# Inverse root as a power on GpSimd, two more row additions on VectorE, more transposes by DMA

## Chip, cores and metric

The kernel runs on one core of a Trainium2 chip. The metric is the device time of one execution in microseconds (us). The engines are TensorE (PE, with its weight loads PEld), VectorE (DVE in the profile, `V` in the code), ScalarE (ACT, `A`), GpSimd (POOL, `G`) and SyncE (SP, `nc.sync`), which here only issues DMAs. A name with a q behind it (SPq, POOLq, ACTq) is the queue of such issues.

## What is computed

Attention over a sliding window of 128 with 4 sink columns, for 4 batches, 8 heads, 768 positions and head size 64, and then a gated MLP block with a spatial gate over the positions:

```python
keep = is_sink | in_window                       # 0 <= row - column < 128, or column < 4
a = softmax(where(keep, q @ k.T / 8, -1e9))
x = (a @ v), heads side by side                  # 4 x 768 x 512

h = gelu_tanh(x @ w_in)                          # 512 -> 1024
u, v = h[..., :512], h[..., 512:]
v_n = (v - mean(v)) / sqrt(var(v) + 1e-6) * g_ln
v_s = einsum('ts,bsd->btd', w_sg, v_n) + b_sg
out = x + (u * v_s) @ w_out                      # float32, 4 x 768 x 512
```

Inputs and output are float32; the matrix products run in bf16.

## The kernel before

Work is cut into 16 pairs of heads (n = 0 to 15; four pairs make one batch) and 4 MLP blocks (b = 0 to 3, one a batch). The positions are six tiles of 128 rows (`NT` = 6). The order on every engine is written out by hand: each engine runs its instructions in the order of the code, and the string `ORDER` (L717) with `INSIDE` (L712) lists the steps behind block 0.

A pair goes through these steps. `load` (L90) fetches k, q and v by DMA from SP's queue into three raw buffers of each name. `cast` (`ck`, `cq`, `cv`; L101) turns them to bf16 on GpSimd. q and k must then stand with the head dimension on partitions. `columns` (`KA`, `QA`, `QV`; L215) does that by six TensorE transposes and one copy on ScalarE or VectorE; `columns_by_dma` (`TD`; L228) does it by two DMA transposes on SP's queue. Which way a pair takes goes with the order of rows in its load: pairs from `FIRST` on (L88) are loaded row by row and turned by DMA. `score` (`S`; L251) multiplies and takes the exponential on ScalarE, `keep_band` (`m`; L283) sets entries outside the window to zero (group 0 on VectorE, the others on GpSimd), and `values` (`A0`, `A1`; L307) multiplies with v; VectorE divides by the sums, keeps the reciprocals in `rcps` and writes x. The x of a pair is turned for the MLP by TensorE (`turn_x`, `XV`; L337) or by a DMA transpose (`turn_x_by_dma`, `XD`; L352).

A block begins when its four pairs are there. `hidden` (L585) issues 14 units: six `hidden_v` (TensorE, GELU on ScalarE, mean and variance on VectorE) and eight `hidden_u`. Behind unit 7 comes `inverse_root` (L400), which gives 1/sqrt(var + 1e-6) for six values in each partition: a first guess from the bits and three Newton steps, 13 instructions on VectorE. `normalise` (L419) then writes the six tiles of `vn`. The rest of the block is put in a list of fillers that the steps `F` take from between the pairs of the next batch: eight `spatial` (L426; six matmuls, then `gv` and `gT` on VectorE), then six `project` (L458; one tile of 128 output rows each). `project` adds x either on TensorE, by a matmul with the identity, and copies with ScalarE (`by_act`), or it adds x on VectorE; a DMA then stores the rows. `LAST` steps of `INSIDE` run behind the last unit of a block, when `vn` is just being written. In this kernel the two rows that are projected there in each block (rows 3 and 5) are both `by_act`. For block 2 rows 3, 4 and 5 are projected behind the units of block 3, by `fill(3)`.

PSUM gives four banks (`ps_m`) to all of these steps but the scores; a bank is free again when the engine that reads it is done.

No pairs follow block 3. There `open_v` (L363) begins the first three `hidden_v` with the pairs whose x is turned already. `count_good` (L486) counts the reciprocals that are in a plain range, and `total` (L498) sums them over the partitions; if one is not, `general()` computes all again in a safe way. It does not run with these inputs. The last rows are projected by `project` and `project_last` (L440).

## Time and profile before

| | |
|---|---|
| median of 3 runs | 164.64 us (164.34 to 168.64) |
| profiled execution | 163.95 us, its span 162.2 us |
| busy share of the span | PE 94%, DVE 81%, ACT 67%, POOL 49% |
| granted TensorE clock, mean | 0.991 |
| moved by DMA | 31.11 MB, mean 192 GB/s |

The span runs from the first to the last event of the execution on the core; the time of the execution is a little longer. Rows of the trace give a start, a length, engine and line, the operation, what it writes and reads, and in brackets the idle time of the engine before it with what ended that. Lengths of pipelined instructions overlap, so the distance between the starts of two of them is the better price of one. Views that group instructions give the busy time and the mean length in nanoseconds. The view of waits gives the total time waited in us, how many times, and the longest.

### The profile page before, as it was taken

How to read it: one execution, taken by the hardware profiler on the slowest of the kernel's cores; microseconds unless marked ns; L12 is line 12 of the kernel's file. 1: busy time of each engine (PE TensorE's matmuls, PEld its weight loads, DVE VectorE, ACT ScalarE, POOL GpSimd, SP SyncE). 2: the span in 40 equal slices, each digit the busy share in tenths (PEclk: the TensorE clock that was granted, in tenths of full speed). 3: DMA queues.
4: the chain of work that ended last, by engine and by line, in shares of the span. 5: the costliest groups of instructions: out<-in, count | busy, mean ns of one | idle time of the engine just before them, and what ended most of it. 6: DMA issues, size and time to landing. Idle time of an engine off the chain costs nothing.

```text
span 162.2 us, 4449 instructions
## 1 busy us (share of the span) xinstructions
PE 152.6 (94%) x1753; PEld 90.5 (56%) x1753; DVE 131.5 (81%) x323; ACT 109.0 (67%) x148; POOL 79.5 (49%) x114
## 2 busy tenths in 40 slices
PE   3889999999999999999999999999999999999960
PEld 3446574666567666565566655554556645555530
DVE  6857975996999995799989984999999959888840
ACT  3198978879977689798977576679759457611020
POOL 6568680404999989641369949102985100000010
PEclk9999999999999999999999999999999999999996
DMA  4999979999999989999932899999932220031253
GB/s 131 337 341 256 210 99 254 223 293 311 304 234 320 297 235 337 317 233 219 188 113 53 119 239 159 261 232 218 216 73 49 111 87 0 0 147 51 91 208 107
DMA packets 60131, 31.11 MB, mean 192 GB/s; under 512 B 48356, under 2 KB 57080, under 8 KB 60104
## 3 DMA queue, kind: packets, MB, share of 16 engines
q1 hardware_dynamic: 56656, 27.20, 71.1%
q0 software_dynamic: 3024, 3.03, 11.1%
q10 hardware_dynamic: 424, 0.53, 1.0%
q8 instruction: 15, 0.25, 0.7%
q14 instruction: 12, 0.10, 0.2%
HBM read 24.81 MB, written 6.29 MB: 192 GB/s over the span
## 4 chain that ended last, share of the span: by engine, by line
PE 67%; DVE 20%; DMA 5%; issue 2%; SPq 1%; ACT 1%; POOL 1%; DVEq 0%; POOLq 0%; ACTq 0%
PE vs L432 14%; PE o_ps L464 9%; PE av L324 7%; PE hv L370 7%; PE sc L267 7%; PE hu L389 6%; DVE st L381 5%; DMA k_sb<-in_k_dram 5%; DVE vn L422 3%; PE xps L341 3%; DVE gv L435 2%; PE av L330 2%; PE kps L219 2%; PE qps L219 2%; PE hv L377 2%
## 5 line engine op out<-in xcount | busy, mean ns | idle before, releaser
L281 ACT ACTIVATE ex<-sc 128x1024 bf16<-128x1024 f32 x48 | 47.4, 1023 | 12.2 <-PE sc L267 6.3
L432 PE MATMUL vs<-wsgT,vn 128*128 128x384 bf16 x192 | 35.6, 326 | 0.2
L298 POOL TENSOR_SCALAR_AFFINE_SELECT ex<-ex 128x512 bf16<-128x512 bf16 x24 | 17.8, 743 | 14.2 <-ACT ex L281 10.3
L107 POOL CAST k_bf<-k_sb 128x768 bf16<-128x768 f32 x15 | 13.1, 871 | 24.0 <-DMA k_sb<-in_k_dram 21.2
L432 PEld LDWEIGHTS <-vn 128*128 128x128 bf16 x192 | 17.6, 97 | 10.9 <-DVE vn L422 0.7
L464 PE MATMUL o_ps<-w_out_sb,gT 128*128 128x512 bf16 x92 | 23.2, 380 | 0.1
L389 PE MATMUL hu<-xT,w_in_sb 128*128 128x384 bf16 x128 | 22.1, 327 | 0.0
L435 DVE SCALAR_TENSOR_TENSOR gv<-vs,g_sb,b_bc 128x384 bf16<-128x384 f32 x32 | 19.6, 612 | 2.2 <-PE vs L432 1.6
L381 DVE BATCH_NORM_STATS2 st<-v_all 128x6 f32<-128x512 f32 x24 | 16.1, 671 | 3.5 <-ACT v_all L379 3.5
L370 PE MATMUL hv<-w_in_sb,xT 128*128 128x512 bf16 x72 | 18.8, 379 | 0.0
L333 DVE TENSOR_TENSOR x<-av,rcps 128x384 bf16<-128x384 f32 x32 | 17.8, 558 | 1.1
L392 ACT ACTIVATE uT<-hu 128x384 bf16<-128x384 f32 x32 | 15.7, 492 | 4.1 <-PE hu L389 3.7
L379 ACT ACTIVATE v_all<-hv 128x512 f32<-128x512 f32 x24 | 13.2, 599 | 7.5 <-PE hv L377 7.1
L107 POOL CAST q_bf<-q_sb 128x768 bf16<-128x768 f32 x15 | 15.3, 1019 | 4.5 <-DMA q_sb<-in_q_dram 1.9
L438 DVE TENSOR_TENSOR gT<-gv,uT 128x384 bf16<-128x384 bf16 x32 | 15.5, 486 | 2.2 <-DVE gv L435 0.5
L389 PEld LDWEIGHTS <-w_in_sb 128*128 128x128 bf16 x128 | 12.3, 98 | 8.0
L472 ACT COPY o_sb<-o_ps 128x512 f32<-128x512 f32 x11 | 6.3, 593 | 15.4 <-PE o_ps L467 15.3
L267 PE MATMUL sc<-qT,kT 64*128 64x256 bf16 (+2 forms) x384 | 16.0, 256 | 0.5 <-DVE qT L225 0.4
L324 PE MATMUL av<-v_sb,ex 128*128 128x65 bf16 x352 | 16.1, 195 | 0.0
L324 PEld LDWEIGHTS <-ex 128*128 128x128 bf16 x352 | 13.0, 98 | 4.7 <-issue 1.9
L104 POOL CAST v_sb<-v_sb 128x768 bf16<-128x768 f32 x16 | 13.5, 842 | 3.2 <-DMA v_sb<-in_v_dram 3.2
L476 POOL DMA_DIRECT2D out_dram<-o_sb x1 | 0.6, 585 | 29.5 <-DVE o_sb L474 29.5
(91 smaller groups left out, 233.1 us busy)
## 6 DMA issues: line engine op xcount, KB each, us to landing
k_sb<-in_k_dram SPq DMA_DIRECT2D x16, 384.0 KB, 6.7
v_sb<-in_v_dram SPq DMA_DIRECT2D x16, 384.0 KB, 6.0
q_sb<-in_q_dram SPq DMA_DIRECT2D x15, 384.0 KB, 5.6
out_dram<-o_sb SPq DMA_DIRECT2D x22, 256.0 KB, 2.4
wsg_sb<-in_moe_w_sg_dram POOLq DMA_DIRECT2D x2, 576.0 KB, 11.6
w_in_sb<-in_moe_w_in_dram POOLq DMA_DIRECT2D x2, 256.0 KB, 5.1
w_in_sb<-in_moe_w_in_dram POOLq DMA_DIRECT2D x1, 512.0 KB, 5.4
w_out_sb<-in_moe_w_out_dram POOLq DMA_DIRECT2D x1, 512.0 KB, 9.2
```

The costliest lines, as they stand in the source:

```text
L107: eng.tensor_copy(dst.rearrange("p t (h d) -> p h t d", h=2), src)
L267: nc.tensor.matmul(sc[part, 512 * l + w:512 * l + w + n_q], kT[rows, 128 * j + wide * a:128 * j + wide * (a + 1)], qT[rows, 128 * j:128 * ...
L281: A.activation(out=exps[n][:, g, :], in_=sc, func=AF.Exp, scale=scale)
L298: eng.affine_select(out=diag, in_=diag, compare_op=ALU.is_ge, fill=0.0, base=0, pattern=[[0, 2], [0, 2], [1, 128]], channel_multiplier=-1)
L324: nc.tensor.matmul(av[:, m, l, :], probs(j, l, half), v_sb[:, l, j, :], start=first, stop=False)
L333: V.tensor_mul(x_sb[b][:, hp, HT * c:HT * (c + 1), :].rearrange("p i (l d) -> p i l d", l=2), av[:, :, :, 0:64], rcp.to_broadcast([128, HT ...
L370: nc.tensor.matmul(hvs[b, j], xT[b][:, c, 128 * j:128 * (j + 1)], w_in_sb[:, c, DF:], start=(c == 0), stop=False)
L381: V.bn_stats(out=st, in_=v_alls[b][:, j, :])
L389: nc.tensor.matmul(h_ps[:, 0:NH], w_in_sb[:, c, 128 * f:128 * (f + 1)], xT[b][:, c, NH * n:NH * (n + 1)], start=(c == 0), stop=(c == KD - 1))
L432: nc.tensor.matmul(vs[:, 0:NH], vns[b][:, si, 128 * f:128 * (f + 1)], wsgT[:, si, cols], start=(si == 0), stop=(si == NT - 1))
L435: V.scalar_tensor_tensor(out=gv, in0=vs[:, 0:NH], scalar=g_sb[:, f:f + 1], in1=b_bc[:, cols], op0=ALU.mult, op1=ALU.add)
L464: nc.tensor.matmul(o_ps, gTs[b][:, c, rows], w_out_sb[:, c, :], start=(c == 0), stop=(c == KU - 1 and not by_act))
```

## The change

- `inverse_root` keeps its first instruction on VectorE (w = var + 1e-6) and takes w to the power -0.5 in one GpSimd instruction, with a constant tile of -0.5.
- `by_act` holds only row 1: rows 3 and 5 of blocks 0 to 2 add x on VectorE, without the identity matmul and without ScalarE's copy.
- `FIRST` is 11: pair 11 (the twelfth) is loaded row by row and turned by `TD 11`; `KA 11` and `QA 11` go. kT and qT have three buffers in place of two.
- The x of pair 14 (the fifteenth) is turned by `XD 14` in place of `turn_x` on TensorE and ScalarE. `open_v` of block 3 takes the parts of pairs 12 and 13 first, then x of pair 15 is turned, and then the parts of pair 14 are added.
- The steps `TD` stand directly behind their casts; within block 1 `ck 11`, `cq 11` come behind unit 9, and `L 13` behind them and `TD 11`.
- `count_good` runs on GpSimd, a matmul pair and a small ScalarE copy sum over the partitions (`count_columns`), and a second matmul over the 96 columns; both stand inside the last block.
- In block 0 `turn_g` comes one unit after the last `hidden_v`, and the second of three `turn_weights` copies is VectorE's.
- Of block 3's rows, row 0 is stored from GpSimd's queue in place of row 3.

```diff
@@ -71,6 +71,7 @@
     off = consts.tile([128, 512], BF16, name="off")
     off0 = consts.tile([128, 512], BF16, name="off0")
     ones = consts.tile([128, 1], BF16, name="ones")
+    minus_half = consts.tile([128, NT], F32, name="minus_half")
 
     vst = [consts.tile([n_sink, c, 2, 65], BF16, name=f"vst{i}")
            for i, c in enumerate((HP, NP - HP))]
@@ -85,7 +86,7 @@
 
         nc.sync.dma_start(out=gates[:, i, :], in_=behind)
 
-    FIRST = 3 * HP
+    FIRST = 3 * HP - 1
 
     def load(n, which, eng=None, in_rows=False):
         b, hp = divmod(n, HP)
@@ -140,6 +141,7 @@
         V.memset(t[:, :, :, 64:65], 1.0)
     load_sinks(0)
     V.memset(ones, 1.0)
+    V.memset(minus_half, -0.5)
     for t in v_bufs:
         V.memset(t[:, :, :, 64:65], 1.0)
     V.memset(off, 0.0)
@@ -217,7 +219,7 @@
         ps = bank([128, NT, 128], BF16, which + "ps")
         for t in range(NT):
             nc.tensor.transpose(ps[:, t, :], src[:, t, :], iden)
-        dst = work.tile([128, S], BF16, name=which + "T")
+        dst = work.tile([128, S], BF16, name=which + "T", bufs=3)
         o, i = dst.rearrange("c (p t) -> c p t", t=NT), ps.rearrange("c t p -> c p t")
         if eng is A:
             A.copy(o, i)
@@ -229,7 +231,7 @@
 
         for which, Ts in (("k", kTs), ("q", qTs)):
             src = flat.pop((n, which))
-            dst = Ts[n] = work.tile([128, S], BF16, name=which + "T")
+            dst = Ts[n] = work.tile([128, S], BF16, name=which + "T", bufs=3)
             nc.sync.dma_start_transpose(out=dst.rearrange("c (t p) -> c t p", t=NT),
                                         in_=src.rearrange("p t c -> p (t c)"))
 
@@ -400,20 +402,9 @@
     def inverse_root(b):
 
         w = small.tile([128, NT], F32, name="w", bufs=2)
-        h = small.tile([128, NT], F32, name="h", bufs=2)
-        s = small.tile([128, NT], F32, name="s", bufs=2)
-        si = small.tile([128, NT], I32, name="si", bufs=2)
         y = small.tile([128, NT], F32, name="y", bufs=2)
         V.tensor_scalar(out=w, in0=mvs[b][:, :, 1], scalar1=1e-6, scalar2=None, op0=ALU.add)
-        V.tensor_single_scalar(out=si, in_=w.bitcast(I32), scalar=1,
-                               op=ALU.logical_shift_right)
-        V.tensor_scalar(out=h, in0=w, scalar1=-0.5, scalar2=None, op0=ALU.mult)
-        V.tensor_scalar(out=y.bitcast(I32), in0=si, scalar1=-1.0, scalar2=float(0x5f3759df),
-                        op0=ALU.mult, op1=ALU.add)
-        for _ in range(3):
-            V.tensor_mul(s, y, y)
-            V.tensor_mul(s, s, h)
-            V.scalar_tensor_tensor(out=y, in0=s, scalar=1.5, in1=y, op0=ALU.add, op1=ALU.mult)
+        G.tensor_tensor(out=y, in0=w, in1=minus_half, op=ALU.pow)
         rstds[b] = y
 
     def normalise(b, j):
@@ -483,23 +474,34 @@
 
     LEAST, MOST = 1e-20, 1e20
 
+    NR = NP * NT
+
     def count_good():
-        good = small.tile([128, NP * NT * 2], F32, name="good", bufs=1)
-        cnt = small.tile([128, 1], F32, name="cnt", bufs=1)
-        cnt_bf = small.tile([128, 1], BF16, name="cnt_bf", bufs=1)
+
+        big = small.tile([128, 2 * NR], F32, name="big", bufs=1)
+        good = small.tile([128, 2 * NR], F32, name="good", bufs=1)
+        good_bf = small.tile([128, 2 * NR], BF16, name="good_bf", bufs=1)
         all_r = rcps.rearrange("p n c m -> p (n c m)")
-        V.tensor_single_scalar(out=good, in_=all_r, scalar=LEAST, op=ALU.is_gt)
-        V.scalar_tensor_tensor(out=good, in0=all_r, scalar=MOST, in1=good,
-                               op0=ALU.is_lt, op1=ALU.mult)
-        V.tensor_reduce(out=cnt, in_=good, axis=AX.X, op=ALU.add)
-        V.tensor_copy(cnt_bf, cnt)
-        return cnt_bf
-
-    def total(cnt_bf):
+        G.tensor_single_scalar(out=big, in_=all_r, scalar=LEAST, op=ALU.is_gt)
+        G.tensor_single_scalar(out=good, in_=all_r, scalar=MOST, op=ALU.is_lt)
+        G.tensor_mul(good_bf, good, big)
+        return good_bf
+
+    def count_columns(good_bf):
         ps = ps_s.tile([128, 1024], F32, name="cps", tag="s")
-        nc.tensor.matmul(ps[0:1, 0:1], cnt_bf, ones, start=True, stop=True)
+        for i in range(2):
+            nc.tensor.matmul(ps[0:NR, 0:1], good_bf[:, NR * i:NR * (i + 1)], ones,
+                             start=(i == 0), stop=(i == 1))
+
+        cnt = small.tile([NR, 1], BF16, name="cnt", bufs=1)
+        A.copy(cnt, ps[0:NR, 0:1])
+        return cnt
+
+    def total(cnt):
+        tot_ps = ps_s.tile([128, 1024], F32, name="tps", tag="s")
+        nc.tensor.matmul(tot_ps[0:1, 0:1], cnt, ones[0:NR, :], start=True, stop=True)
         tot = small.tile([1, 1], I32, name="tot", bufs=1)
-        V.tensor_copy(tot, ps[0:1, 0:1])
+        V.tensor_copy(tot, tot_ps[0:1, 0:1])
         return tot
 
     def general():
@@ -595,13 +597,13 @@
         gate = [[lambda f=f, n=n: spatial(b, f, n) for f in range(KU)] for n in range(2)]
         if b < B - 1:
             fillers.extend(gate[0] + gate[1])
-            by_act = (1, 3, 5)
+            by_act = (1,)
             order = (0, 2, 4, 1, 3, 5) if b < B - 2 else (1, 0, 2, 3, 4, 5)
             fillers.extend(lambda ends=None, t=t: project(b, t, t in by_act, ends) for t in order)
             return
 
 
-        rows = [lambda t=t: project(b, t, t in (0, 4), store=G if t == HT else nc.sync)
+        rows = [lambda t=t: project(b, t, t in (0, 4), store=nc.sync if t else G)
                 for t in range(NT - 1)]
         fillers.extend(gate[0] + [gate[1][0], rows[0], gate[1][1], gate[1][2], rows[1],
                                   gate[1][3]] + rows[2:])
@@ -695,8 +697,8 @@
         open_v(0, j, (2,))
     load_all(HP + 3)
     between = {NT + 1: [lambda: columns(HP, "k", A)], NT + 3: [lambda: columns(HP, "q", A)],
-               NT + 4: [turn_g],
-               NT + 2 * KU - 1: [lambda si=si: turn_weights(si, A) for si in range(3)]}
+               NT: [turn_g],
+               NT + 2 * KU - 1: [lambda si=si: turn_weights(si, V if si == 1 else A) for si in range(3)]}
     hidden(0, between)
     cast_all(HP + 1)
     load_w_out()
@@ -710,8 +712,8 @@
 
     LAST = NT + 2 * KU - 1
     INSIDE = {
-        1: {1: "A0 8", 3: "A1 8", 5: "KA 9", 6: "L 12, L 13", 7: "QA 9", 9: "XD 8",
-            LAST: "ck 11, cq 11, cv 10, S 9 0 1, F 1, QV 10, F 1"},
+        1: {1: "A0 8", 3: "A1 8", 5: "KA 9", 6: "L 12", 7: "QA 9",
+            9: "XD 8, ck 11, cq 11, TD 11, L 13", LAST: "cv 10, S 9 0 1, F 1, QV 10, F 1"},
         2: {1: "A0 12", 3: "A1 12", 6: "L 15, L 16", 9: "XD 12", LAST: "S 13 0 1, F 2"},
     }
     ORDER = """
@@ -724,16 +726,16 @@
         ck 9, cq 9, cv 8, F 1, XV 6,
         L 11, S 8 0 1, A0 7, m 8 1, D, S 8 2, m 8 2, A1 7, E, m 8 0, ck 10, cq 10, cv 9,
         O 1 0, O 1 1, XV 7, O 1 2, B 1,
-        m 9 0 1, F 1, KA 10, F 1, S 9 2, m 9 2, ck 12, cq 12, F 1,
-        S 10 0 1, A0 9, m 10 0 1, F 1, KA 11, S 10 2, m 10 2, A1 9, XD 9, TD 12, L 14,
-        F 1, QA 11, cv 11, ck 13, cq 13, F 1,
-        S 11 0 1, A0 10, m 11 0 1, F 1, S 11 2, m 11 2, A1 10, TD 13, F 1, cv 12, ck 14, cq 14,
+        m 9 0 1, F 1, KA 10, F 1, S 9 2, m 9 2, ck 12, cq 12, TD 12, F 1,
+        S 10 0 1, A0 9, m 10 0 1, F 1, S 10 2, m 10 2, A1 9, XD 9, L 14,
+        F 1, cv 11, ck 13, cq 13, TD 13, F 1,
+        S 11 0 1, A0 10, m 11 0 1, F 1, S 11 2, m 11 2, A1 10, F 1, cv 12, ck 14, cq 14, TD 14,
         F 1, XV 10,
-        S 12 0 1, A0 11, m 12 1, F 1, S 12 2, m 12 2, A1 11, TD 14, F 1, m 12 0, cv 13, F 1,
+        S 12 0 1, A0 11, m 12 1, F 1, S 12 2, m 12 2, A1 11, F 1, m 12 0, cv 13, F 1,
         O 2 0, O 2 1, XV 11, O 2 2, B 2,
         ck 15, m 13 0 1, cq 15, F 2, S 13 2, m 13 2, TD 15, cv 14, F 1,
         S 14 0 1, A0 13, m 14 0 1, F 1, S 14 2, m 14 2, A1 13, XD 13, F 1, cv 15, F 1,
-        S 15 0 1, A0 14, m 15 0 1, F 1, S 15 2, m 15 2, A1 14, F 1, G, F 1
+        S 15 0 1, A0 14, m 15 0 1, F 1, S 15 2, m 15 2, A1 14, XD 14, F 1, G, F 1
     """
 
     ends = []
@@ -781,17 +783,18 @@
     run(ORDER)
     values(NP - 1, 0)
     fill()
-    turn_x(NP - 2, A)
     values(NP - 1, 1)
     fill(len(fillers) - 3)
-    open_v(B - 1, 0)
-    open_v(B - 1, 1)
+    for j in range(3):
+        open_v(B - 1, j, (0, 1))
     turn_x(NP - 1, V)
-    open_v(B - 1, 2)
+    for j in range(3):
+        open_v(B - 1, j, (2,))
     seen = {}
     hidden(B - 1, {2: [lambda: seen.update(c=count_good())],
+                   NT: [lambda: seen.update(c=count_columns(seen["c"]))],
+                   NT + 4: [lambda: seen.update(t=total(seen["c"]))],
                    LAST: [lambda: fill(3)]})
-    seen["t"] = total(seen["c"])
     fill(4)
     count = nc.values_load(seen["t"][0:1, 0:1], min_val=0, max_val=128 * NP * NT * 2)
     fill(len(fillers) - 3)
```

## Prediction

> **What bounds the kernel now.** I read the busy shares first, then the chain that ended last, then a table of stretches, and then the rows where two blocks join.
>
> ```profile
> PE 152.6 (94%) x1753; PEld 90.5 (56%) x1753; DVE 131.5 (81%) x323; ACT 109.0 (67%) x148; POOL 79.5 (49%) x114
> PE 67%; DVE 20%; DMA 5%; issue 2%; SPq 1%; ACT 1%; POOL 1%; DVEq 0%; POOLq 0%; ACTq 0%
> 64.00:79.00 15.00, 15.00 (x124) 8.62 (x123) 13.46 (x40) 12.75 (x21) 6.14 (x8) 1.00 1.20 259
> 79.00:98.00 19.00, 19.00 (x287) 11.75 (x286) 17.53 (x37) 13.41 (x16) 14.57 (x20) 1.00 0.77 137
> ```
>
> The last two rows give, for a stretch, its length and the busy time of PE, PEld, DVE, ACT and POOL. TensorE is busy for all of each stretch, and the granted clock (the third number from the end) is 1.00. VectorE is behind it at 90% and 92%. So an instruction taken from TensorE is worth its length, as long as VectorE does not become late. The waits of the weight loads from 36 to 157 us show how little TensorE waits for data:
>
> ```profile
> PEld L432 <- DVE vn L422: 0.7, 3, 0.4
> PEld L464 <- DVE gT L438: 0.7, 2, 0.6
> ```
>
> VectorE's fifth of the chain lies where a block ends its statistics and must write `vn`. These are the joints of blocks 1, 2 and 3:
>
> ```profile
> 72.81 0.72 DVE L407 TENSOR_SCALAR w<-mv 128x6 f32<-128x6 f32 x1
> 75.78 2.83 DVE L422 TENSOR_SCALAR vn<-v_all,mv,y 128x512 bf16<-128x512 f32 x6
> 78.66 1.14 PE L432 MATMUL vs<-wsgT,vn 128*128 128x384 bf16 x6
> 107.58 0.17 DVE L407 TENSOR_SCALAR w<-mv 128x6 f32<-128x6 f32 x1
> 110.58 2.83 DVE L422 TENSOR_SCALAR vn<-v_all,mv,y 128x512 bf16<-128x512 f32 x6
> 112.42 2.35 PE L432 MATMUL vs<-wsgT,vn 128*128 128x384 bf16 x12
> 134.76 0.23 DVE L491 TENSOR_SCALAR good<-rcps 128x192 f32<-128x192 f32 x1
> 135.88 0.68 DVE L381 BATCH_NORM_STATS2 st<-v_all 128x6 f32<-128x512 f32 x1
> 138.40 0.17 DVE L407 TENSOR_SCALAR w<-mv 128x6 f32<-128x6 f32 x1
> 140.83 2.83 DVE L422 TENSOR_SCALAR vn<-v_all,mv,y 128x512 bf16<-128x512 f32 x6
> 142.90 5.05 PE L432 MATMUL vs<-wsgT,vn 128*128 128x384 bf16 x30
> 144.24 0.60 DVE L435 SCALAR_TENSOR_TENSOR gv<-vs,g_sb,b_bc 128x384 bf16<-128x384 f32 x1
> ```
>
> From w to the first `vn` are 2.97, 3.00 and 2.43 us, spent in twelve tiny instructions.
>
> **TensorE's share of the change.** These rows price what goes:
>
> ```profile
> 140.55 0.38 PE L467 MATMUL o_ps<-x,iden 128*128 128x512 bf16 x1
> 140.77 1.89 PE L464 MATMUL o_ps<-w_out_sb,gT 128*128 128x512 bf16 x8
> 84.54 0.34 PE kps L219 x6
> 127.40 0.34 PE xps L341 x6
> 142.80 0.16 PE L500 MATMUL cps<-ones,cnt_bf 128*1 128x1 bf16 x1
> ```
>
> An identity matmul occupies TensorE from 140.55 to 140.77, 0.22 us. Six go (rows 3 and 5 of three blocks): 1.32 us. Eighteen transposes go (k of pair 11 at 84.54, its q, and x of pair 14 at 127.40): 3 x 0.34 = 1.02 us. The count gets two small matmuls more than the one at 142.80, at up to 0.16 each: I take +0.1 for both (0 to 0.3). Together -2.24 us, all in stretches where TensorE is full.
>
> **The power.** No GpSimd power stands in the trace. Call its time P. It is bounded below by the smallest GpSimd instruction, and above by GpSimd taking twelve steps, as VectorE does, each as long as its large select:
>
> ```profile
> L817 POOL MEMSET const-float32-0.0<- 128x1 f32 x1 | 0.1, 98 | 0.3 <-issue 0.3
> masks.py:199 POOL TENSOR_SCALAR_AFFINE_SELECT iden<-iden 128x128 bf16<-128x128 bf16 x1 | 0.3, 287 | 0.1
> L298 POOL TENSOR_SCALAR_AFFINE_SELECT ex<-ex 128x512 bf16<-128x512 bf16 x24 | 17.8, 743 | 14.2 <-ACT ex L281 10.3 <-issue 1.9 <-DMA out_dram<-o_sb 1.5
> ```
>
> That is 0.1 to 12 x 0.743 = 8.9 us. I take 1.0: the 0.29 of a small GpSimd instruction and some 0.1, a whole memset, for each of six columns. That is nearer to the lower row, since it is one instruction over six columns and not over 512. Handing over to GpSimd and back I estimate at 0.1 each way, half of what two dependent small steps on VectorE lie apart (2.43 over twelve).
>
> When does `vn` come then, and when does TensorE need it? The first `vs` takes the six tiles one after another, so the last is needed 0.81 us behind its start (five of six steps of 0.16).
>
> Block 1: w is done at 72.98 (the 0.72 is a wait, below), y at 73.2+P, the last `vn` at 76.0+P. TensorE comes there 0.44 earlier than 78.66 and needs it at 79.0. Block 2: 107.75, 107.95+P, 110.8+P, needed at 112.8. Block 3: the count leaves VectorE, which brings the later statistics from 135.88 to 134.8, and TensorE is 0.34 earlier, so w is done at 137.1, y at 137.3+P, the last `vn` at 140.1+P, needed at 142.9. With P = 1.0 TensorE waits for `vn` nowhere. It waits from P = 2.0 on in block 2 and 2.8 in the others. Of the 1.4 us of waits in the two rows above I count 0.9 as regained (0 to 1.4), most of it in blocks 2 and 3. In block 0 the copy of weights that VectorE takes from ScalarE fits into an idle 0.93 of VectorE:
>
> ```profile
> 38.30 1.49 DVE L206 COPY wsgT<-wps 128x768 bf16<-128x768 bf16 x3 [0.93 <-PE wps L201]
> 38.77 1.39 PE L432 MATMUL vs<-wsgT,vn 128*128 128x384 bf16 x6
> ```
>
> The first `vs` takes 1.39 here and 1.14 at 78.66; that difference is worth 0.2 (0 to 0.7). `turn_g` is moved within full work and costs nothing either way.
>
> **The additions on VectorE.** They stand behind `vn` and ahead of the first `gv`.
>
> ```profile
> 143.57 0.69 DVE L474 TENSOR_TENSOR o_sb<-o_ps,x 128x512 f32<-128x512 f32 x1
> ```
>
> Two more of 0.69 are 1.38 us at each of three joints. The Newton steps give back 2.97-0.2-P in block 1, so VectorE is even at P = 1.4. In block 3 it did one of the three rows already, at 143.57: `vn` ends at 141.1 for P = 1.0, three rows bring it to 143.0, and the first `vs` is done at 143.1. Before, `gv` began at 144.24. What waits behind the additions is `gv`, and behind that TensorE, for a bank: three of the four can be filled before it stops. I put nothing on this, and 0 to 1.5 us for the range. The stores of these rows wait for the additions on SP's queue; next behind them is `TD 12`, whose casts come only behind the masks of pair 9.
>
> **The port that GpSimd and VectorE share.** w at 72.81 took 0.72 instead of 0.17, and ended as this cast did:
>
> ```profile
> 72.67 0.83 POOL L104 CAST v_sb<-v_sb 128x768 bf16<-128x768 f32 x1
> ```
>
> In the change the three casts of block 1 stand on GpSimd's queue behind the power, so they run beside `vn`. No row has `vn` beside a cast. At worst each cast holds VectorE 0.83: 2.5 us. The slack at P = 1.0 is 79.0-77.0 = 2.0. I charge 0.2 (0 to 1.5 with block 2's one cast).
>
> The Trainium skill (SBUF — State Buffer, "Who interferes with whom") names `tensor_scalar` among the operations that can take both ports and then exclude GpSimd for a whole instruction. By that rule `vn`, a `tensor_scalar` between two SBUF tiles, is held up by each cast; the sum would be 0.5 higher than mine. The wait at 72.81 agrees for w; for `vn` no run here shows it.
>
> **The queues.** A DMA transpose holds SP some 1.25 us, and its data is in use within 4.3 us of the issue:
>
> ```profile
> k_sb<-in_k_dram SPq DMA_DIRECT2D x16, 384.0 KB, 6.7
> 116.77 1.24 SPq L233 DMA_TRANSPOSE qT<-q_bf  x1
> 121.06 0.61 PE L267 MATMUL sc<-qT,kT 64*128 64x256 bf16 x8
> 89.00 0.95 POOL L107 CAST k_bf<-k_sb 128x768 bf16<-128x768 f32 x1
> 125.66 0.56 DVE L333 TENSOR_TENSOR x<-av,rcps 128x384 bf16<-128x384 f32 x1
> 130.60 0.81 PE L370 MATMUL hv<-w_in_sb,xT 128*128 128x512 bf16 x3
> ```
>
> `TD 11` waits for the casts behind the power (75.8), issues until 78.3, and `L 13` follows; with 6.7 us to land its k is there at 85, and is cast at 89.0. x of pair 14 is written at 126.2 and by the same 4.3 turned at 130.5 at the latest; TensorE takes it behind the other parts and the turning of x of pair 15, at 130.3, near where the third part of `hv` stands now (130.60). Both are hidden with little to spare, and a third buffer of kT and qT keeps `TD 11` from waiting for pair 9. SP gets `L 14` sooner, as it no longer stands behind the two transposes of pair 12 and the casts they wait for. That is worth nothing, since the casts of pair 14 had TensorE's other work beside them. The row from GpSimd's queue ended no later than the last:
>
> ```profile
> 155.88 0.58 POOL L476 DMA_DIRECT2D out_dram<-o_sb  x1 [29.50 <-DVE o_sb L474]
> 157.30 0.38 ACTq L456 DMA_DIRECT2D out_dram<-o_last  x1
> ```
>
> So its move is worth nothing. The count on GpSimd reads sums that are there at 129, with GpSimd idle until 155.88.
>
> **Sum.** 163.95 - 2.24 - 0.9 - 0.2 + 0.2 = 160.8 us for the profiled execution. The runs shown stand at 164.34 and 164.64, up to 0.7 above it; I predict 161.0, 2.2% under the median. Small changes under 2% count as no change here, so the result lies close to that line.
>
> **Rivals.** (1) A slow power, slower than before: beyond P = 2.0 to 2.8 each microsecond is lost in every block, since nothing else is queued on VectorE ahead of `vn`. P = 4.5, half of the upper bound, costs 2.5 us in block 2 (115.3 against 112.8), 1.5 in block 1 (80.5 against 79.0) and 3.4 in block 3, where three rows behind `vn` bring `gv` to 146.5 and the first `vs` was done at 143.1: 161.0+7.4 = 168.4. For it speaks that no such instruction is priced here; against it, that it has only six columns. From P = 3.1 it eats the whole gain. (2) VectorE is late at the joints though the power is quick: P near 1.5, full lock-out by casts and the additions uncovered. The regained 1.1 is lost and 1 us added: 163.0. For it: 92% busy from 79 to 98. Against: three free banks. (3) Something paid once at the first power. The nearest row is ScalarE's table load, 1.28 us; block 0 has that much room (its `vn` starts at 34.48, 2.4 behind its w if it goes as block 3 does), so 161.0 stays; if it were 4 to 6 us, `vn` of block 0 would be 0 to 2 us late: up to 163.0.
>
> The Trainium skill (GPSIMD Engine Reference, "Instruction dispatch") states about 6 us for the first call of a freshly loaded GpSimd routine. By that rule the time would be near 163; no run here shows such a load.
>
> ```profile
> L379 ACT ACT_TABLE_LOAD x3 | 3.8, 1283 | 0.1
> 34.48 1.92 DVE L422 TENSOR_SCALAR vn<-v_all,mv,y 128x512 bf16<-128x512 f32 x4
> ```
>
> (4) A DMA transpose is late (`TD 11` or `XD 14`) by 1 to 2 us: 162.5. Rows 116.77 and 121.06 speak against it.
>
> **How the numbers follow.** The forecast has 0.55, (1) 0.20, (2) 0.15, (3) as a real delay 0.04, (4) 0.06. The forecast's own range is 159.2 to 162.6, from the bounds of the regained waits (0.5 more from `vn` and `gT`, 0.5 from block 0, and what the runs lie below or above) and of the lock-out. The range 158.8 to 165.6 takes in (2) to (4) and the mild part of (1), P up to some 3.5. Faster by over 2% takes 0.46 of the forecast and 0.04 of the others, slower by over 2% takes 0.20, the rest is no change.
>
> **What would show it.** Right: one power a block of near 1 us with `vn` starting 1.2 to 1.7 us behind w; no L467 in rows 3 and 5; TensorE still busy in every stretch; and its busy time some 2 us smaller. Wrong: a power of over 2.7 us with PE waiting for `vn`; a `vn` stretched beyond 2.83 by casts; waits of `sc` or `hv` for a DMA transpose; or `gv` late behind L474.

## The result and the profile after

The changed kernel takes 164.05 us, the median of 22 runs, against 164.85 us for the kernel before in as many: a ratio of 0.9952 [0.993, 0.9974] (in brackets the 95% interval). That is half a per cent faster and counts as no change here. 161.0 us were predicted. The profiled execution took 164.03 us, with a span of 162.0 us, 0.2 us less than that of before: the profiled pair shows less of the gain than the medians do, since the profiled execution of before (163.95 us) was 0.9 us quicker than its median. All ratios are of undisturbed executions; the profiled executions of e5, e12, e13 and e15 were longer ones, so of their traces only the end is read.

The page of the changed kernel, busy times and the chain that ended last:

```profile
PE 150.3 (93%) x1713; PEld 89.9 (55%) x1731; DVE 128.8 (79%) x279; ACT 103.0 (64%) x139; POOL 87.2 (54%) x121
PE 45%; DVE 23%; issue 11%; POOL 10%; DMA 3%; ACT 3%; SPq 1%; POOLq 0%; ACTq 0%; DVEq 0%
```

TensorE lost 2.3 us of busy time, as the prediction had it (2.24). But its part of the chain fell from 67% to 45%: GpSimd, which held 1%, has 10%, and VectorE more than before. The same stretches of the changed kernel, with the columns of before:

```profile
64.00:79.00 15.00, 14.90 (x122) 8.62 (x123) 12.37 (x28) 12.76 (x22) 8.06 (x10) 1.00 1.14 216
79.00:98.00 19.00, 18.46 (x272) 10.91 (x273) 18.51 (x40) 11.31 (x12) 15.88 (x22) 1.00 1.11 201
113.50:129.00 15.50, 15.01 (x220) 8.95 (x220) 15.01 (x33) 9.08 (x11) 11.34 (x16) 1.00 0.49 95
```

TensorE now idles 0.54 us from 79 to 98 and 0.49 from 113.5 to 129, where VectorE is busy for 97%. The kernel before, in the last of these stretches (a row that the prediction did not read):

```profile
113.50:129.00 15.50, 15.50 (x229) 9.46 (x230) 15.00 (x32) 10.83 (x14) 10.04 (x15) 1.00 0.55 106
```

VectorE was at 15.00 of 15.50 there already. It had no room for more rows.

The power, as a group (minimum, median and maximum in ns), and the joint of block 1 in the timeline of the changed kernel:

```profile
L407 POOL TENSOR_TENSOR y<-w,minus_half x4: 1323/1348/1363, 32.6 to 137.1; 128x6 f32<-128x6 f32 x4
```

```profile
73.08 0.17 DVE L406 TENSOR_SCALAR w<-mv 128x6 f32<-128x6 f32 x1
73.34 1.34 POOL L407 TENSOR_TENSOR y<-w,minus_half 128x6 f32<-128x6 f32 x1 [5.34 <-DVE w L406]
74.66 0.81 POOL L108 CAST k_bf<-k_sb 128x768 bf16<-128x768 f32 x1
74.72 4.33 DVE L413 TENSOR_SCALAR vn<-v_all,mv,y 128x512 bf16<-128x512 f32 x6 [1.47 <-POOL y L407]
75.42 1.02 POOL L108 CAST q_bf<-q_sb 128x768 bf16<-128x768 f32 x1
76.39 1.02 POOL L105 CAST v_sb<-v_sb 128x768 bf16<-128x768 f32 x1
78.50 1.14 PE L423 MATMUL vs<-wsgT,vn 128*128 128x384 bf16 x6
78.97 0.67 DVE L465 TENSOR_TENSOR o_sb<-o_ps,x 128x512 f32<-128x512 f32 x1
79.57 0.94 DVE L227 COPY qT<-qps 128x768 bf16<-128x768 bf16 x1
80.44 0.67 DVE L465 TENSOR_TENSOR o_sb<-o_ps,x 128x512 f32<-128x512 f32 x1
80.56 1.14 PE L423 MATMUL vs<-wsgT,vn 128*128 128x384 bf16 x6 [0.37 <-DVE qT L227]
81.63 0.60 DVE L426 SCALAR_TENSOR_TENSOR gv<-vs,g_sb,b_bc 128x384 bf16<-128x384 f32 x1
```

The power is quick, 1.35 us, and `vn` begins 1.64 us behind the start of w, against 2.97 before. But beside three casts `vn` takes 4.33 us instead of 2.83 and ends at 79.05 instead of 78.61. Then come an addition, the copy of qT and the next addition, and TensorE's second `vs` waits for the bank that this copy empties. Counted from the first `hv` of block 1 (63.42 after, 63.15 before), this second `vs` begins at 17.14 us against 16.83, although TensorE has less work ahead of it.

In block 2, and behind it:

```profile
109.20 3.31 DVE L413 TENSOR_SCALAR vn<-v_all,mv,y 128x512 bf16<-128x512 f32 x6 [1.44 <-POOL y L407]
112.00 2.11 PE L423 MATMUL vs<-wsgT,vn 128*128 128x384 bf16 x12
114.23 0.60 DVE L426 SCALAR_TENSOR_TENSOR gv<-vs,g_sb,b_bc 128x384 bf16<-128x384 f32 x1
126.32 1.04 PE L455 MATMUL o_ps<-w_out_sb,gT 128*128 128x512 bf16 x4 [0.44 <-DVE x L335]
```

Here the gain shows: the two `vs` that began at 112.42 in the kernel before, and took 2.35 us there with waits inside, now take 2.11. A part of it is given back at 126.32, where TensorE waits for VectorE's x.

At the end, the last matmul and SP's wait behind its branch; first before, then after:

```profile
156.59 0.27 PE L454 MATMUL o_ps<-x,iden 128*128 128x256 bf16 x1
SPq L800 <- SPq L800: 2.7, 5, 1.2
```

```profile
155.59 0.27 PE L445 MATMUL o_ps<-x,iden 128*128 128x256 bf16 x1
SPq L803 <- SPq L803: 2.5, 2, 2.0
```

The second kind of row gives the sum, the number and the longest wait. The matmuls end 1.0 us earlier, yet the span ends only 0.2 us earlier. What lies behind the last matmul, called the tail below, grew from 5.37 to 6.14 us, and SP has one wait of 2.0 us behind its branch (the jump over `general()`), where the longest was 1.2. Two other things changed on SP by the trace: its last whole-row store takes 1.12 us to issue instead of 0.33, and a packet of 8192 bytes on the instruction queue q14 falls at 156.68; the nearest before the branch was at 146.8 in the kernel before.

The semaphores and landings in the trace tell what the wait of 2.0 us is. A DMA signals its landing by a semaphore. The stores on SP's and ScalarE's queues take eight of them in turn, and behind the branch SP waits for all eight, one by one, in an order that is the same in every kernel here. In the changed kernel the last whole row has the first semaphore of that order: its data lands at 159.38 us, and the wait ends at 159.40. In the kernel before, the last three stores have the last three places, so the first wait is over after 0.48 us and the long ones come later. The tail so has two parts: the last landing comes 3.97 us behind the last matmul (3.65 before), and from there to the end it is 2.17 us (1.72 before), because six waits for semaphores that are done already still follow, 0.07 to 0.09 us each. Of the 0.77 us, 0.45 are this order and 0.32 a later landing.

A ledger of TensorE, from the start of the first `hv` of a block to that of the next (block 3: to the end of the last matmul), each read from the timeline of one execution; e1 to e4 are the first experiments:

| us | before | after | e1 | e2 | e3 | e4 |
|---|---|---|---|---|---|---|
| block 1 and the pairs behind it | 34.80 | 34.54 | 34.52 | 33.95 | 34.19 | 34.41 |
| block 2 and the pairs behind it | 31.02 | 30.63 | 30.64 | 30.65 | 30.46 | 31.56 |
| block 3 | 27.89 | 27.27 | 27.27 | 27.27 | 27.70 | 27.59 |
| tail | 5.37 | 6.14 | 6.27 | 6.28 | 5.80 | 6.43 |

Blocks 2 and 3 agree within 0.03 us between traces with the same code there. The column of before is less firm elsewhere: e11, which has the same code from block 1 on, has 35.14 in block 1 and a tail of 5.71.

### The profile page after: what moved, and what is told of

It reads as the page before. It is cut to its first block, busy times and chain, and to the rows that moved or that the text cites. A ratio compares the mean times of both kernels' runs of the same rounds, so it can differ in the third digit from the quotient of the medians.

```text
span 162.0 us, 4332 instructions
## 1 busy us (share of the span) xinstructions
PE 150.3 (93%) x1713; PEld 89.9 (55%) x1731; DVE 128.8 (79%) x279; ACT 103.0 (64%) x139; POOL 87.2 (54%) x121
## 4 chain that ended last, share of the span: by engine, by line
PE 45%; DVE 23%; issue 11%; POOL 10%; DMA 3%; ACT 3%; SPq 1%; POOLq 0%; ACTq 0%; DVEq 0%
PE vs L423 9%; PE hu L391 7%; PE o_ps L455 6%; PE hv L372 5%; DVE gv L426 4%; DVE gT L429 4%; DVE vn L413 4%; PE sc L269 3%; PE av L326 3%; DMA q_sb<-in_q_dram 3%; ACT ex L283 2%; DVE x L335 2%; POOL ex L300 2%; POOL ex L302 2%; PE kps L221 2%
## 5 line engine op out<-in xcount | busy, mean ns | idle before, releaser
L300 POOL TENSOR_SCALAR_AFFINE_SELECT ex<-ex 128x512 bf16<-128x512 bf16 x24 | 18.6, 773 | 10.4 <-ACT ex L283 10.4
L455 PE MATMUL o_ps<-w_out_sb,gT 128*128 128x512 bf16 x83 | 22.2, 379 | 0.9 <-DVE x L335 0.4
L413 DVE TENSOR_SCALAR vn<-v_all,mv,y 128x512 bf16<-128x512 f32 x24 | 13.3, 619 | 5.9 <-POOL y L407 5.9
L108 POOL CAST q_bf<-q_sb 128x768 bf16<-128x768 f32 x15 | 14.7, 981 | 3.3 <-DMA q_sb<-in_q_dram 2.4
L407 POOL TENSOR_TENSOR y<-w,minus_half 128x6 f32<-128x6 f32 x4 | 5.4, 1345 | 20.0 <-DVE w L406 20.0
```

Source lines behind the costliest of these rows:

```text
L108: eng.tensor_copy(dst.rearrange("p t (h d) -> p h t d", h=2), src)
L300: eng.affine_select(out=diag, in_=diag, compare_op=ALU.is_ge, fill=0.0, base=0, pattern=[[0, 2], [0, 2], [1, 128]], channel_multiplier=-1)
L455: nc.tensor.matmul(o_ps, gTs[b][:, c, rows], w_out_sb[:, c, :], start=(c == 0), stop=(c == KU - 1 and not by_act))
```

## The experiments

Unless another kernel is named, each edit is made to the changed kernel, and each ratio is to the kernel before.

**e1: the row store back.**

```diff
-        rows = [lambda t=t: project(b, t, t in (0, 4), store=nc.sync if t else G)
+        rows = [lambda t=t: project(b, t, t in (0, 4), store=G if t == HT else nc.sync)
```

> The changed kernel with row 3 of the last block stored from GpSimd's queue again and row 0 from SP's. Theory (SP's queue at the end): the changed kernel finished its matmuls 1.0 us earlier than before, but its span ended only 0.2 earlier, since three stores of 256 KB now stand behind each other on SP and the last half row went out at 156.74 as before (156.95). Then this kernel is 0.5 to 0.8 us quicker than the changed one: ratio to before 0.991 (0.989 to 0.993), with the last store of SP issued near 156.0 or earlier. Rival (the end is set by the last transfer and the closing steps, whatever queue): no difference, 0.995, and the last SP store still near 156.7.

Measured: 0.9964 [0.9937, 0.999], tail 6.27 us. Which row GpSimd's queue stores does not matter, and it is not what made the tail longer.

**e2: the casts of block 1 ahead of the power.**

```diff
-        1: {..., 6: "L 12", 7: "QA 9", 9: "XD 8, ck 11, cq 11, TD 11, L 13", LAST: "cv 10, S 9 0 1, ..."},
+        1: {..., 6: "L 12, QA 9, ck 11, cq 11, cv 10", 9: "XD 8, TD 11, L 13", LAST: "S 9 0 1, ..."},
```

> The changed kernel with the three casts ck 11, cq 11 and cv 10 of block 1 ahead of the power on GpSimd's queue (QA 9 comes one unit earlier for it). Theory (the casts hold VectorE's port): the six vn tiles take 2.83 us in block 1 instead of 4.33, the 0.74 us that TensorE waits at the second vs goes, and the kernel is 0.5 to 0.8 us quicker than the changed one: ratio to before 0.991. Rival (the two additions ahead of gv make VectorE late, the casts do not matter): vn still ends near 79, or the wait at the second vs stays above 0.5 us; ratio 0.995.

The joint of block 1 in its timeline, and the stretch behind it:

```profile
75.14 2.82 DVE L413 TENSOR_SCALAR vn<-v_all,mv,y 128x512 bf16<-128x512 f32 x6 [1.47 <-POOL y L407]
78.19 0.69 DVE L465 TENSOR_TENSOR o_sb<-o_ps,x 128x512 f32<-128x512 f32 x1 [0.23 <-PE o_ps L455]
80.50 1.14 PE L423 MATMUL vs<-wsgT,vn 128*128 128x384 bf16 x6
79.00:98.00 19.00, 19.00 (x278) 11.31 (x277) 18.51 (x38) 12.00 (x14) 14.74 (x20) 1.00 1.08 200
```

`vn` is back at 2.82 us, VectorE now waits for TensorE at 78.19, and the second `vs` begins without a wait. TensorE is busy for all of 79 to 98, although the two additions are still VectorE's. Block 1 is 0.59 us shorter (33.95 against 34.54), and blocks 2 and 3 do not move. The ratio is 0.9929 [0.9907, 0.9951], an interval that overlaps that of the changed kernel: the 0.59 rest on the traces. So the casts beside `vn` cost 1.5 us on VectorE and 0.6 on TensorE. The Trainium skill's rule (SBUF — State Buffer, "Who interferes with whom"), left open in the prediction for `vn`, is borne out: three casts lengthened it by 1.5 us, the one cast of block 2 by 0.48 (3.31). The trace has it one by one: three of the six `vn` instructions of block 1 overlap a cast and take 1.04 us each, the other three take 0.53.

**e3: rows 3 and 5 back to ScalarE and the identity matmul.**

```diff
-            by_act = (1,)
+            by_act = (1, 3, 5)
```

> The changed kernel with rows 3 and 5 of blocks 0 to 2 on TensorE and ScalarE again (identity matmul and copy). TensorE has 1.32 us more to do. Theory (VectorE's additions cost what they save): the waits of 0.74 us at the second vs of block 1 and 0.61 us at 126 go, so the kernel is 0 to 0.4 us slower than the changed one: ratio to before 0.995 to 0.998. Rival (the casts cause the wait in block 1, the additions are free): the wait in block 1 stays and the kernel is 1.0 to 1.3 us slower than the changed one: ratio 1.001 to 1.003, slower than before.

Its two stretches:

```profile
79.00:98.00 19.00, 19.00 (x278) 11.32 (x277) 18.34 (x38) 12.52 (x15) 16.17 (x22) 1.00 1.22 202
113.50:129.00 15.50, 15.50 (x225) 9.23 (x223) 14.91 (x32) 10.02 (x13) 10.54 (x16) 1.00 0.53 102
```

TensorE is full again in both. The ledger has it 0.35 shorter in block 1, 0.17 shorter in block 2 and 0.43 longer in block 3: the sum, -0.09, is nothing. The ratio is 0.9963 [0.9931, 0.9994], the same as with the change. The six identity matmuls that were taken off TensorE, 1.32 us, came back as waits for VectorE in blocks 1 and 2. In block 3, where VectorE has room (it is busy for 10.71 of 14.00 us from 129 to 143), they are a gain. In block 1 the wait that goes here is the one that e2 ended by moving the casts, so it takes the casts and the additions together; no run gives these rows back beside e2.

**e4: the Newton steps back on VectorE** (lines 407 to 416 of before in place of the power).

```diff
-        G.tensor_tensor(out=y, in0=w, in1=minus_half, op=ALU.pow)
+        ...
```

> The changed kernel with the Newton steps on VectorE in place of the power. Theory (the power takes 1.35 us and gives VectorE back 0.8 to 1.1 us a block, of which block 1 loses all to casts that run beside vn): block 1 is no later than with the power, blocks 2 and 3 are 0.3 to 0.8 us later each, together 0.5 to 1.2 us slower than the changed one: ratio to before 0.998 to 1.003. Rival (the power is worth nothing, because TensorE has other work at the joints): within 0.2 us of the changed one, 0.994 to 0.996.

Measured: 1.0035 [1.0009, 1.0061]. So the power is worth some 0.8%: 0.93 us in block 2, 0.32 in block 3, and by the ledger nothing in block 1 (34.41 against 34.54), where it comes with casts beside `vn` and the Newton steps came without (`vn` at 76.53 for 2.82).

**e7: the additions alone.** The kernel before with `by_act = (1,)` and nothing else.

```diff
-            by_act = (1, 3, 5)
+            by_act = (1,)
```

> The kernel before with one part of the change: rows 3 and 5 of blocks 0 to 2 add x on VectorE. TensorE has 1.32 us less to do. Theory (VectorE is late at the joints with the Newton steps and cannot take 1.38 us more): the first gv of each block comes 0.9 to 1.4 us later than before, TensorE loses more than the 1.32 us to waits for banks, and the kernel is 0.3 to 1.3 us slower than before: ratio 1.002 to 1.008. Rival (three free banks cover the additions, as the prediction put it): 0.8 to 1.3 us quicker, ratio 0.992 to 0.995.

```profile
79.00:98.00 19.00, 18.27 (x280) 11.38 (x281) 17.99 (x38) 12.64 (x14) 14.01 (x19) 1.00 0.72 123
113.50:129.00 15.50, 14.62 (x210) 8.61 (x212) 15.05 (x32) 9.63 (x11) 10.53 (x15) 1.00 0.52 113
```

The ratio is 1.0096 [1.007, 1.0123]: alone, this part makes the kernel 1% slower. TensorE has 1.4 us less work (151.2 against 152.6) and idles 0.73 and 0.88 us in the two stretches. The cover that the prediction counted on, "three of the four can be filled before it stops", was not enough.

**e5 and e6: six and twelve more small DMAs on SP's queue in block 0.** They were to move the packet of q14 away from the tail.

```diff
+    extra = consts.tile([1, 6, 8], F32, name="extra")      # e6: 12
+    for i in range(6):                                     # e6: 12
+        nc.sync.dma_start(out=extra[:, i, :], in_=off0[0:1, 0:16].bitcast(F32))
     hold_loads(0, w_in_sb[0:1, 0, DF:DF + 16].bitcast(F32))
```

> The changed kernel with six more DMAs of 32 bytes on SP's queue at 16 us, where SP waits anyway. They only move every later instruction of SP back by six places. Theory (SP's instruction fetch): in all changed kernels so far one SP issue of the last rows takes 0.9 to 1.5 us instead of 0.33, with a block of instructions fetched at that moment, and SP's branch over the rarely run part is followed by a gap of 1.7 to 2.3 us (0.48 before); in the kernel before, that block was fetched at 146.6, where SP sat idle. If six places are enough to move the fetch to SP's idle time near 146 to 152, the long issue and most of the gap go, the time from the last matmul to the end of the span falls from 6.14 to 5.4, and the ratio to before is 0.990 to 0.992. If not, the fetch moves to an earlier store and the tail shrinks by 0.3 or less. Rival (the end is set by transfers): tail 6.1 to 6.3, ratio 0.995 or a little above, for the time of six more DMAs.

> The same with twelve more DMAs of 32 bytes on SP's queue. Theory (SP's instruction fetch): the fetch lies before 152 us, in SP's idle time; no SP issue of the last rows above 0.6 us; the tail behind the last matmul is 5.3 to 5.6 us instead of 6.14; ratio 0.990 to 0.992. Rival: tail 6.1 to 6.3, ratio 0.995 to 0.997.

Six: 0.9897 [0.987, 0.9923], quicker than the changed kernel. But its trace has the packet still in the tail, 0.55 us behind the last matmul, and a tail of 5.79 us. Twelve: 1.0255 [1.0186, 1.0324], a median of 169.0 us, some 5 us slower than the changed kernel, and that has a plain cause. SP of the changed kernel waits 5.8 us in block 0 before it issues pair 4's loads (at 21.6 us); six DMAs, 4.8 us in all (e5), fit into this wait, and twelve, 9.0 us (e6), do not. k of pair 4 is issued at 24.8 in e6, and TensorE stops for its cast; this is in its waits:

```profile
PE kps L221 <- POOL k_bf L108: 3.2, 1, 3.2
```

The first wait behind SP's branch, called the pause below, did fall to 0.48 us, and yet the tail of e6 was 6.20 us: with twelve more DMAs the last three stores have places five to seven of the eight in the order of waits, and the last of them lands 4.34 us behind the last matmul.

**e8: e2 with rows 3 and 5 of block 1 given back, and twelve DMAs.**

```diff
-            by_act = (1,)
+            by_act = (1, 3, 5) if b == 1 else (1,)
```

> The changed kernel with three repairs: the casts of block 1 ahead of the power, rows 3 and 5 of block 1 (projected at the joint of block 2) on TensorE and ScalarE again, and the twelve small DMAs on SP. From the traces: 0.6 us from the casts in block 1, 0.1 to 0.2 from block 2 (its 0.61 us wait ahead of block 3 goes, 0.43 of matmuls come back), 0.6 to 0.8 from the tail: 1.3 to 1.6 us quicker than the changed kernel, ratio to before 0.986 to 0.988. If the tail is not SP's fetch: 0.990 to 0.992.

Measured: 1.0156 [1.013, 1.0181], spoiled by the twelve as e6 was: the first `vs` of block 0 begins at 44.55 us instead of 39.01. Its pause behind the branch is 0.48 us, its tail 5.94.

**e9: the same without the DMAs**, so e2 and this:

```diff
-            by_act = (1,)
+            by_act = (1, 3, 5) if b == 1 else (1,)
```

> The changed kernel with the casts of pairs 11 and 10 in block 1 ahead of the power (as in e2_casts_first) and with rows 3 and 5 of block 1 alone given back to ScalarE and the identity matmul. Theory (VectorE is the limit where block 1's rows are added, its work there costs more than the matmuls): block 1 stays 0.6 us shorter than in the changed kernel, the next stretch 0.2 us shorter; matmuls end near 155.3, ratio to before near 0.991. Rival (the two edits gain the same time): no quicker than e2_casts_first, ratio 0.993.

Measured: 0.9933 [0.9911, 0.9956], blocks 33.95, 30.45 and 27.27 us, tail 6.04. The 0.2 us of block 2 are in the trace; beside e2 the time shows nothing.

**e10: e9, with the last whole row on GpSimd's queue too.**

```diff
-        rows = [lambda t=t: project(b, t, t in (0, 4), store=nc.sync if t else G)
+        rows = [lambda t=t: project(b, t, t in (0, 4), store=G if t in (0, 4) else nc.sync)
```

> As e9_casts_and_rows, and row 4 of block 3, the last whole row, is stored from GpSimd's queue too, so that SP issues only the half row behind it. Theory (the changed kernel's longer tail, 6.1 us from the last matmul to the end against 5.4, comes from SP's last whole store, which takes 1.1 us to issue and holds back the half row): the tail is back at 5.3 to 5.6 us, 0.6 us quicker than e9_casts_and_rows, ratio near 0.987. Rival (SP's pause behind its branch sets the end, whatever it stores): tail 6.0 to 6.3, ratio as e9_casts_and_rows.

Measured: 0.994 [0.9914, 0.9967], tail 6.75 us. The theory fell. SP's half-row store now takes the 1.12 us itself, and the pause behind the branch is the longest of all. It is the wait for that half row, which has the first semaphore of the order and lands last, at 159.30 us; all other waits still follow:

```profile
155.08 1.12 SPq L447 DMA_DIRECT2D out_dram<-o_last  x1
SPq L803 <- SPq L803: 3.0, 1, 3.0
```

**e11: the six DMAs in the kernel before.**

```diff
+    extra = consts.tile([1, 6, 8], F32, name="extra")
+    for i in range(6):
+        nc.sync.dma_start(out=extra[:, i, :], in_=off0[0:1, 0:16].bitcast(F32))
     hold_loads(0, w_in_sb[0:1, 0, DF:DF + 16].bitcast(F32))
```

> The kernel before with six more DMAs of 32 bytes on SP's queue in block 0, as e5_sp_six_more had them. Theory (the six do something in block 0, a pause on SP that keeps its loads from colliding, and have nothing to do with the tail): also 0.5% quicker than the kernel before, ratio 0.995. Rival (they gained by moving SP's instruction fetch out of the tail): the tail of before is short already, so nothing is gained, ratio 0.998 to 1.004.

Measured: 0.9982 [0.9956, 1.0008]. No gain that can be told from none. Its trace has 1.84 us from the last landing to the end, where the kernel before had 1.72.

**e12 and e13: e9 with the six DMAs in block 0**, twice; the edit to e9 is the one shown for e11.

> As e9_casts_and_rows, with the six small DMAs of e5_sp_six_more. If the six are worth what e5_sp_six_more showed beside the changed kernel (0.55%), ratio 0.985 to 0.987. If that was only the difference between two sets of runs, the same as e9_casts_and_rows, near 0.991.

> The kernel of e12_casts_rows_six once more, beside the two below. Ratio 0.986 if its gain is real; if its trace loses nothing in block 0, the trace shows where the 1.1 us against e9_casts_and_rows lie: in block 0 (the first matmul of block 1 at 62.7 instead of 63.8) or behind the last matmul (tail of 5.0 instead of 6.0).

Measured: 0.986 [0.9822, 0.9898] and 0.9845 [0.9781, 0.991]. The gain beside e9 is there again. The traces do not show its place; their tails are 5.95 and 6.15 us, of which 1.72 and 1.96 lie behind the last landing (e9: 2.18).

**e14 and e15: e9 with six or twelve DMAs ahead of block 3**, where SP issues nothing for 12 us.

```diff
+    extra = consts.tile([1, 6, 8], F32, name="extra")      # e15: 12
+    for i in range(6):                                     # e15: 12
+        nc.sync.dma_start(out=extra[:, i, :], in_=off0[0:1, 0:16].bitcast(F32))
     seen = {}
```

> As e9_casts_and_rows, with the six small DMAs not in block 0 but ahead of block 3, at 130 to 134 us, where SP issues nothing. Theory (they gain by their number, since they shift which of SP's instructions the fetch falls on at the end): the same gain as in block 0, ratio 0.986. Rival (they gain by their place, since SP's loads come some microseconds later in block 0): no gain, ratio 0.992 to 0.994.

> As e14_six_late, with twelve, until 138 us. Theory of the fetch: the pause behind SP's branch falls to 0.5 us and the tail to 5.4, ratio 0.988 or less. Rival (neither the pause nor the fetch sets the tail): the pause falls to 0.5 us as in e6_sp_twelve_more, and the tail stays near 6.0, ratio 0.992 to 0.994.

Measured: 0.9834 [0.9752, 0.9916] and 0.9854 [0.9765, 0.9943]. The gain is there from another place too, so it doesn't hang on block 0. e14 has the lowest ratio here, 162.71 us in the median beside 165.27 for the kernel before, though e12, e13 and e15 cannot be told from it. The interval of its ratio lies wholly below that of the changed kernel. Its last matmul and SP's wait:

```profile
154.72 0.27 PE L445 MATMUL o_ps<-x,iden 128*128 128x256 bf16 x1
SPq L806 <- SPq L806: 1.8, 1, 1.8
```

Tail: 5.45 us, against 6.04 in e9, though the pause is 1.8 us long. e15, whose pause is 0.48 us, has 5.46. Neither the pause nor its absence sets the tail by itself: 0.48 us went with tails of 5.37 to 6.20, and 2.0 to 2.3 us with 5.79 to 6.43. In every trace with a pause over 0.48 us it ends within 0.02 us of the landing that the first semaphore signals.

The two parts of the tail, by the place of the store that lands last in SP's order of waits (the order has eight places; e6 and e8 have twelve small DMAs more than the changed kernel, e5 and e12 to e14 six, e15 twelve):

| place of the last landing | kernels | from the last matmul to this landing, us | from there to the end, us |
|---|---|---|---|
| first | e10 | 4.17 | 2.58 |
| second | changed, e1, e2, e3, e4, e9 | 3.64 to 4.25 | 2.17 to 2.18 |
| sixth | e6, e8, e11, e15 | 3.60 to 4.34 | 1.84 to 1.86 |
| seventh | e7 | 4.02 | 1.78 |
| eighth | before, e5, e12, e13, e14 | 3.53 to 4.23 | 1.72, in e13 and e14 1.96 and 1.92 |

So the place sets the second part nearly to the tenth of a microsecond. (In e13 and e14 the first semaphore was signalled only 0.30 and 0.35 us before the last landing, so the waits between were still going on.) What sets the first part is not shown.

## Why the prediction was wrong, step by step

- *TensorE's share, -2.24 us: right in busy time* (152.6 to 150.3), *wrong as a gain*. It held as long as "VectorE does not become late"; for the six rows' 1.32 us VectorE was late (e3, e7).
- *The additions at 0: the step that failed most.* The prediction looked at VectorE from 64 to 98, at 90 and 92%, and not from 113.5 to 129, where it was at 97%. In the changed kernel they eat what they save, some 1.3 us, inside of the bound of 1.5 (e3); alone, with the Newton steps still on VectorE, they make the kernel some 1.6 us slower, 1.3 saved and 2.9 lost (e7). In block 1 of the changed kernel they do so only together with the casts: with these out of the way TensorE is full there (e2).
- *The charge of 0.2 us for the casts: too small.* Block 1 lost 0.59 us to them (e2), within the bound of 1.5, and the sign that the prediction gave for its being wrong, "a `vn` stretched beyond 2.83 by casts", was there. (The 0.5 us that the prediction puts on full lock-out is 2.5 less the slack of 2.0; beside a sum that holds the 0.2 already it would be 0.3.) `vn` ended at 79.05, as the assumed need of 79.0 allows; what was late was the work queued behind it, the additions and the copy of qT. The slack was counted for `vn` alone.
- *The regained waits, 0.9 us: about half.* The waits within the two `vs` of block 2 and a wait for `gT` in block 3 went, 0.5 us in all by the timelines; 0.44 came back at 126.32.
- *Block 0, -0.2 us: nothing.* The first `vs` takes 1.39 us there as before, and block 1 begins 0.27 us later (63.42 against 63.15).
- *The tail: not in the sum at all.* It was taken to stay as it was, and grew by 0.77 us in the profiled executions: 0.45 by the place of the last stores in SP's order of waits, 0.32 by a later landing.
- *The power: right.* 1.35 us lies between the value taken, 1.0, and the 2.0 from which it would have held TensorE; `vn` starts 1.64 behind w, with 1.2 to 1.7 forecast. Rival (1) is out. So is rival (3): the four powers take 1323 to 1363 ns, the first among them. By the rule of the Trainium skill (GPSIMD Engine Reference, "Instruction dispatch") the first call of a freshly loaded routine would cost some 6 us; this trace does not show it.
- *The transposes by DMA, the count and the row store: right.* No wait of TensorE names a DMA transpose, and e1 prices the store at nothing.

What came is rival (2), given 0.15: VectorE late at the joints, the power near 1.5 us, casts that hold `vn` up (by 1.5 us of the 2.5 at worst), and uncovered additions. It was priced at 163.0 us. The tail was in no rival's price, so that 163.0 with the tail's 0.8 comes close to 164.05 is in part luck.

By the ledger the sum is this. For the three blocks the forecast was 2.24 + 0.9 - 0.2 = 2.94 us gained, and they gained 0.26 + 0.39 + 0.62 = 1.27: 1.67 short. Block 1 was to begin 0.2 earlier and began 0.27 later: 0.47. The tail grew by 0.77. Together 2.91 us are missing: the span was to be 3.14 shorter and is 0.23 shorter. The 1.67 cannot be divided cleanly between additions, casts and waits, since in block 1 additions and casts are the same wait.

Open stays what sets the time from the last matmul to the last landing (3.53 to 4.34 us), and most of what six small DMAs take off the mended kernel (e9), some 0.8%, and not off the kernel before. A part of that follows from the order of waits: six more DMAs move the last landing from the second place to the eighth in the mended kernel, which is worth 0.22 to 0.46 us, and from the eighth to the sixth in the kernel before, which costs 0.12. Of e14's 1.05 us of span against e9, 0.59 is tail (0.26 by the order, 0.33 by the landing); the rest is in block 0, where TensorE waits 0.55 us for the DMA of `wsg_sb` in e9 and not in e14. This wait differs between executions of the same code (0.55 in e9, 0.08 in e10), so it need not come from the six DMAs.

## What to carry to other kernels

Work taken from a full engine is a gain only where the engine that takes it over has room in that stretch: read its busy share stretch by stretch, and leave none of the stretches out that the work is put into. Slack counted for one instruction must also hold for everything queued behind it on its engine. And an end of matmuls that comes earlier is not yet an earlier end of the kernel; the work behind the last one belongs in the sum, with the order in which the last stores are waited for.

## What was not expected of the hardware

- A GpSimd power of 128x6 float32 takes 1.32 to 1.36 us, the first like the rest.
- GpSimd's casts beside VectorE's `vn` cost both: `vn` 4.33 us instead of 2.83, two casts 1.02 instead of the 0.83 that they take without `vn` beside them (e2).
- Behind the branch at the end, SP pauses 0.48 us in some kernels (before, e6, e7, e8, e11, e15) and 1.4 to 3.0 in the others. The long pauses are waits for a store: the stores of SP's and ScalarE's queues take eight semaphores in turn, SP waits for them in a fixed order, and in these kernels the first of the order belongs to one of the last stores (in the changed kernel it lands at 159.38 us, and the pause ends at 159.40). Six or twelve DMAs more on SP's queue, in block 0 or ahead of block 3, move the last stores on by as many places, counted round the eight. What the 0.48 us are, which pass where the first store has long landed, no run here shows.
